# Attention weights kept in float32 for the AV product, and weight loads issued from POOL's queue

## The chip, the cores and the metric

The kernel runs on one core of a Trainium2 chip. A core has a matrix engine (TensorE, PE in the profile, with its weight loads shown as PEld), a vector engine (VectorE, DVE), a scalar engine (ScalarE, ACT), a general one (GpSimd, POOL) and a queue engine (SyncE, SP). Each works through its own instructions in order, and semaphores tie them together. Data lie in on-chip memory of 128 partitions; PE writes its results to a separate accumulation memory (PSUM). DMAs are issued from a queue of SP, ACT or POOL. The metric is device time in microseconds (us) of one execution.

## The reference

Four batches, eight heads, 768 positions, head size 64. Attention is restricted to clusters: every query and key is assigned to the nearest of 16 centroids of its head, and a query sees the keys of its own cluster only. The result goes through an MLP whose middle step mixes positions.

```python
mask = q_assign[:, :, :, None] == k_assign[:, :, None, :]
scores = scale * np.matmul(q, k.transpose(0, 1, 3, 2))
scores = np.where(mask, scores, -1000000000.0)
scores = scores - np.max(scores, axis=-1, keepdims=True)
attn = np.exp(scores)
attn = attn / (np.sum(attn, axis=-1, keepdims=True) + 1e-09)
attn_out = np.matmul(attn, v)
# x: the heads of attn_out side by side, (4, 768, 512)
h = np.maximum(x @ w_in, 0.0)              # w_in 512 x 1024
u, v = h[..., :512], h[..., 512:]
v_n = (v - mean(v)) / np.sqrt(var(v) + 1e-06)
v_s = np.einsum('ts,bsd->btd', w_spatial, v_n) + b_spatial[None, :, None]
return (u * v_s) @ w_out                   # w_out 512 x 512
```

All inputs and outputs are float32.

## The kernel before

Every float32 operand of a matrix product is split in two float16 halves, high and low, and a product is made of three of the four half-products: high-high, high-low and low-high. They accumulate in PSUM.

The work goes by pairs of heads, 16 pairs in all (four to a batch). For a pair, `prep` (L476) loads q, k and V, splits them, computes the cluster logits on PE (L508 to L510), turns them into one-hot rows on DVE and copies these as extra rows beside q, so that the mask is part of the score product. `shifts` (L577) runs the scores once (tile `tps`, one PSUM buffer, L587), takes each query's maximum on DVE (`nm`, L590), and lays the shift, again as extra rows, beside q. `attend` (L606) then does, for each of two heads, six key blocks: scores (tile `sc`, L622 and L624), exp on ACT into the float32 tile `p32` (L627), a cast to float16 on ACT (L628) and the low half on POOL (L629), both into `pt`. With all six blocks there, six AV blocks of 128 queries follow on PE (L638): for every key block three half-products of 65 columns (64 of V and a one, for the sum of the weights), with the weights as the stationary operand, and last a product with the tile `mean`, which adds the mean of V for rows where nothing is seen. The division (L653 to L655), the split of x (cast on DVE L657, low half on POOL L658) and a transposing DMA from SP (L660) put x into the buffer of its batch.

V is loaded to a staging tile `vraw` and split by ACT (L547) and DVE (L548). Its sum over positions is taken by PE: twelve matmuls with ones (L555, L556). DVE splits that (L564, L565), and two small DMAs put it in `mean`.

The MLP of a batch (`mlp`, L668) is 324 matmuls of 512 columns, all of L678, three half-products each. Its weights are loaded once, in 36 pieces; of a piece ACT makes the high half (L419, L440) and DVE the low one (L424, L445); for `w_in` and `w_out` DVE first puts the words of a float64 together (L434 to L436). The loads are issued from ACT's queue.

The order of all engines is worked out when the program is built: the class `Plan` (L114) simulates the queues with a cost for each step, and of the steps that are ready at a time it takes the one with the lowest key. Attention steps have small keys. The steps of the MLP on PE have keys from `FILLER` up, so they are taken only where nothing else is ready. The order on the chip is then fixed: an engine that waits for one instruction does not take a later one.

Of the kernel before, what the change touches and what calls it, by code (L numbers as in the profile page):

```python
# [7 lines left out]
F32 = mybir.dt.float32  # L8
F16 = mybir.dt.float16
# [6 lines left out]
P = 128  # L16
# [4 lines left out]
P_LOG = 10  # L21
V_SCALE = 2.0 ** 6
X_LOG = 10
# [5 lines left out]
PEN = 2.0 ** 15  # L29
MEAN_UNIT = 2.0 ** -2  # L30
LN2 = 0.6931471805599453
# [5 lines left out]
R_OH, R_SH, R_E, R_END = 64, 80, 81, 83  # L37
P32_BUFS = 3
PT_BUFS = 9
HQ_BUFS = 3  # L40
V_BUFS = 2
# [8 lines left out]
W_GAP = 4.0  # L50
W_ON = ('ACT',)
W_POOL = False
W_HI_DVE = ()
# [191 lines left out]
def kernel(  # L245
# [62 lines left out]
    r_raw = R(wk, "raw", [P, 2, S], F32, 1)  # L308
    r_vraw = R(wk, "vraw", [P, NT, P], F32, 1)
# [3 lines left out]
    r_pt = R(wk, "pt", [P, 2, S], F16, PT_BUFS)  # L313
    r_xhl = R(wk, "xhl", [P, NT, 2, P], F16, 1)
# [7 lines left out]
    r_nm = R(sm, "nm", [P, 2, NT], F32, 2)  # L322
    r_wh = R(sm, "wh", [2, 2, D + 2], F16, 2)
    r_wl = R(sm, "wl", [2, 2, D + 2], F16, 2)
    r_rc = R(sm, "rc", [P, NT], F32, 2)
# [150 lines left out]
    def prep(n):  # L476
# [5 lines left out]
        KV = PREP_KEY + 3.0  # L482
        raw, vraw = r_raw.new(), r_vraw.new()
# [50 lines left out]
        for x in range(4):  # L534
# [10 lines left out]
            else:  # L545
                rows.append(sp(lambda dst=dst, src=src: nc.sync.dma_start(out=dst(), in_=src()), 0.1, after=[tr, lg] + qa0, use=[hq, oht], key=KP))
        o_vh = op("ACT", 0.84, lambda: A.activation(out=vh.t[:, :, :, 0:D], in_=vraw.t.rearrange("p t (h d) -> p t h d", d=D), func=AF.Copy, scale=V_SCALE), after=[ldv, c_one], use=[vraw], new=[vh], key=KV)  # L547
        o_vl = op("DVE", 1.16, lambda: V.scalar_tensor_tensor(out=vh.t[:, :, :, D + 2:], in0=vraw.t.rearrange("p t (h d) -> p t h d", d=D), scalar=V_SCALE, in1=vh.t[:, :, :, 0:D], op0=ALU.mult, op1=ALU.subtract), after=[o_vh], use=[vraw, vh], key=KV)  # L548

        sv = r_acc.new()  # L550

        def sums():
            o = sv.t[:, 0:2 * (D + 2)].rearrange("p (h d) -> p h d", h=2)
            for t in range(NT):
                T.matmul(out=o[:, :, 0:D + 1], lhsT=ones, rhs=vh.t[:, t, :, 0:D + 1], start=(t == 0), stop=False, skip_group_check=True)  # L555
                T.matmul(out=o[:, :, 0:D], lhsT=ones, rhs=vh.t[:, t, :, D + 2:], start=False, stop=(t == NT - 1), skip_group_check=True)  # L556

        o = op("PE", 0.75, sums, after=[o_vh, o_vl, c_wt], use=[vh], new=[sv], cols=1548, key=KV)
        wh, wl = r_wh.new(), r_wl.new()

        def svr():
            return sv.t[0:2, 0:2 * (D + 2)].rearrange("p (h d) -> p h d", h=2)[:, :, 0:D + 1]

        h_ = op("DVE", 0.25, lambda: V.tensor_scalar(out=wh.t[:, :, 0:D + 1], in0=svr(), scalar1=MEAN_UNIT, scalar2=None, op0=ALU.mult), after=[o], use=[sv], new=[wh], key=KV)  # L564
        l_ = op("DVE", 0.3, lambda: V.scalar_tensor_tensor(out=wl.t[:, :, 0:D + 1], in0=svr(), scalar=MEAN_UNIT, in1=wh.t[:, :, 0:D + 1], op0=ALU.mult, op1=ALU.subtract), after=[h_], use=[sv, wh], new=[wl], key=KV)  # L565
        w1 = sp(lambda: nc.sync.dma_start(out=mw.t[R_E:R_E + 1, :, 0:D + 1], in_=wh.t[0:1, :, 0:D + 1]), 0.05, after=[h_, c_mean], use=[wh], new=[mw], key=KV)
        w2 = sp(lambda: nc.sync.dma_start(out=mw.t[R_E + 1:R_E + 2, :, 0:D + 1], in_=wl.t[0:1, :, 0:D + 1]), 0.05, after=[l_, c_mean], use=[wl, mw], key=KV)
        X["rows"] = rows + qa0
        X["go"] = rows + qa0 + [qa1, lo1]
        X["v"] = [o_vh, o_vl, w1, w2]  # L570

# [5 lines left out]
    def shifts(n):  # L577
# [22 lines left out]
        a = op("DVE", 0.2, lambda: V.tensor_scalar(out=cols(0, 1), in0=nmv(1), scalar1=PEN * PEN / 4, scalar2=1.0 / PEN, op0=ALU.min, op1=ALU.mult), after=tops + [c_sh], use=[nm], new=[sx], key=K_SH)  # L600
        e = op("DVE", 0.2, lambda: V.tensor_scalar(out=cols(1, 2), in0=nmv(2), scalar1=PEN * PEN / 2, scalar2=None, op0=ALU.is_gt), after=tops + [c_sh], use=[nm, sx], key=K_SH)
        tr = sp(lambda: nc.sync.dma_start_transpose(sht.t, sx.t.rearrange("p t c -> p (t c)")), 0.67, after=[a, e], use=[sx], new=[sht], turn=True, key=K_SH)
        X["shift"] = [sp(lambda h=h: nc.sync.dma_start(out=hq.t[R_SH:R_END, 1, h, :], in_=sht.t[R_SH + 16 * h:R_SH + 16 * h + 3].rearrange("c t s -> c (t s)")), 0.1, after=[tr], use=[hq, sht], key=K_SH) for h in range(2)]


    def attend(n):  # L606
# [5 lines left out]
        for h in range(2):  # L612
            pts, los = [], []
            for k in range(NT):
                sc, p32, pt = r_sc.new(), r_p32.new(), r_pt.new()
                pts.append(pt)

                def scores(sc=sc, h=h, k=k):
                    ks = slice(k * P, (k + 1) * P)
                    cols = (slice(0, 512), slice(512, S))  # L620
                    for cs in cols:
                        T.matmul(out=sc.t[:, cs], lhsT=lo.t[:, h, ks], rhs=hq.t[:, 2, h, cs], start=True, stop=False)  # L622
                    for cs in cols:
                        T.matmul(out=sc.t[:, cs], lhsT=hq.t[0:R_E, 0, h, ks], rhs=hq.t[0:R_E, 1, h, cs], start=False, stop=True)  # L624

                o = op("PE", 0.65, scores, after=X["go"] + X["shift"], use=[hq, lo], new=[sc], cols=2 * S, key=K_SC)
                o = op("ACT", 0.99, lambda sc=sc, p32=p32: A.activation(out=p32.t, in_=sc.t[:, 0:S], func=AF.Exp, bias=plog, scale=SC_UNIT), after=[o, m_half], use=[sc], new=[p32], key=K_EXP)  # L627
                o = op("ACT", 0.83, lambda pt=pt, p32=p32: A.copy(out=pt.t[:, 0, :], in_=p32.t), after=[o], use=[p32], new=[pt], key=K_HI)  # L628
                los.append(op("POOL", 1.7, lambda pt=pt, p32=p32: G_.tensor_tensor(out=pt.t[:, 1, :], in0=p32.t, in1=pt.t[:, 0, :], op=ALU.subtract), after=[o], use=[p32, pt], key=K_LO))  # L629
            av = r_acc.new()  # L630
            prev = None
            for t in range(NT):
                def values(av=av, pts=pts, h=h, t=t):
                    ts = slice(t * P, (t + 1) * P)
                    c = t * (D + 1)

                    def mm(w, lhsT, rhs, **k):
                        T.matmul(out=av.t[:, c:c + w], lhsT=lhsT, rhs=rhs, skip_group_check=True, **k)  # L638
# [7 lines left out]
                prev = op("PE", 0.62, values, after=los + X["v"] + [prev], use=pts + [vh, mw, hq] + ([av] if t else []), new=[] if t else [av], cols=18 * 65, key=AV_KEY)  # L646
            rc, xn = r_rc.new(), r_xn.new()
            f = 2.0 ** (6 - X_LOG)

# [6 lines left out]
            hs = slice(h * D, (h + 1) * D)  # L656
            o = op("DVE", 0.45, lambda xn=xn, hs=hs: V.tensor_copy(out=xhl.t[:, :, 0, hs], in_=xn.t), after=[o], use=[xn] + ([xhl] if h else []), new=[] if h else [xhl], key=K_X)  # L657
            xls.append(op("POOL", 1.0, lambda xn=xn, hs=hs: G_.tensor_tensor(out=xhl.t[:, :, 1, hs], in0=xn.t, in1=xhl.t[:, :, 0, hs], op=ALU.subtract), after=[o], use=[xn, xhl]))  # L658
# [162 lines left out]
```

## Time and profile before

| | |
|---|---|
| Median of 2 runs | 802.5 us (798.8 to 806.21) |
| The profiled execution | 808.25 us, its span 806.4 us |
| Mean granted clock of PE | 0.937 |
| PE busy | 669.5 us (83%) |
| DVE busy | 538.0 us (67%) |
| POOL busy | 430.5 us (53%), 330.9 of it L629 |
| ACT busy | 400.3 us (50%), 170.3 of it L627 and 152.7 L628 |

The profile is that of one execution. A row of a group gives line, engine, operation, tiles (out<-in), shape and count, then busy time in us, the mean of one in ns, and idle time ahead of them with what ended it. A row in order of time starts with start and length in us. A row of waits names who waited for whom, then us in total, how often, and the longest. The granted clock is 1 at full speed; it falls to half where PE has had little work. Busy times of PE hold the time until a result is written, so a busy PE may still have room. Before its first change the granted clock is shown as 1.

### The profile page before, as it was taken

What the parts mean: (1) busy time and instruction counts of PE and PEld (TensorE: products, weight loads), DVE (VectorE), ACT (ScalarE), POOL (GpSimd) and SP (SyncE); (2) the same over time, 40 slices, a digit from 0 to 9 for tenths busy, and PEclk for the clock granted to TensorE, in tenths of its full rate; (3) what the DMA queues carried; (4) which work ended last, traced back from release to release, by engine and by line L of the source; (5) the groups of instructions that cost most, each with busy time, mean ns of one, the idle gap of its engine ahead of it and who ended that gap; (6) DMA issues with size and microseconds to landing.
All of it is one profiled execution on the core that took longest, in us unless ns stands there. A gap on an engine that the chain in (4) does not pass through costs nothing. (4 is left out here: it accounts for less than half of the span.)

```text
span 806.4 us, 16781 instructions
## 1 busy us (share of the span) xinstructions
PE 669.5 (83%) x6865; PEld 398.6 (49%) x6865; DVE 538.0 (67%) x898; ACT 400.3 (50%) x541; POOL 430.5 (53%) x296
## 2 busy tenths in 40 slices
PE   2236867767678978999888979997999999999997
PEld 1113545444445554565655646555655655444443
DVE  6587797869896888677777787949767425312411
ACT  2016666637275647467737564766566771012111
POOL 1005665637374675758848385968476883212311
PEclk9999778767788999999999999999999999999999
DMA  4751144535243154054437240416412211121023
GB/s 154 166 139 53 37 115 113 141 80 164 59 118 51 30 112 122 16 72 136 84 108 157 67 106 18 119 26 152 99 42 57 64 48 21 27 79 53 12 52 92
DMA packets 96472, 67.74 MB, mean 84 GB/s; under 512 B 79310, under 2 KB 82060, under 8 KB 96396
## 3 DMA queue, kind: packets, MB, share of 16 engines
q1 hardware_dynamic: 87468, 51.34, 27.7%
q10 hardware_dynamic: 8928, 15.34, 5.9%
q8 instruction: 53, 0.87, 0.5%
q14 instruction: 23, 0.19, 0.1%
HBM read 27.63 MB, written 6.29 MB: 42 GB/s over the span
## 5 line engine op out<-in xcount | busy, mean ns | idle before, releaser
L629 POOL TENSOR_TENSOR pt<-p,pt 128x768 f16<-128x768 f32 x192 | 330.9, 1745 | 192.7 <-ACT pt L628 180.9
L590 DVE TENSOR_REDUCE nm<-tps 128x1 f32<-128x768 f32 x192 | 182.5, 950 | 94.2 <-PE tps L587 93.5
L627 ACT ACTIVATE p<-sc,plog 128x768 f32<-128x768 f32 x192 | 170.3, 900 | 86.1 <-PE sc L624 58.6
L587 PE MATMUL tps<-hq 80*128 80x512 f16 (+1 forms) x384 | 107.5, 366 | 90.2 <-DVE nm L590 79.0
L628 ACT CAST pt<-p 128x768 f16<-128x768 f32 x192 | 152.7, 830 | 34.4 <-PE acc L638 25.3
L638 PEld LDWEIGHTS <-pt 128*128 128x128 f16 x3456 | 132.9, 102 | 17.7 <-issue 4.5
L678 PE MATMUL acc<-win,xT 128*128 128x512 f16 x576 | 135.0, 386 | 2.5 <-DVE xn L655 2.2
L638 PE MATMUL acc<-vhl,pt 128*128 128x65 f16 (+1 forms) x3456 | 136.0, 199 | 0.5 <-POOL pt L629 0.5
L622 PE MATMUL sc<-hq,lo 128*128 128x512 f16 (+1 forms) x384 | 104.5, 356 | 10.6 <-ACT p L627 10.5
L624 PE MATMUL sc<-hq 81*128 81x512 f16 (+1 forms) x384 | 103.7, 354 | 6.2 <-DMA hq<-sht 6.2
L587 PEld LDWEIGHTS <-hq 80*128 80x128 f16 x384 | 37.9, 103 | 132.4 <-issue 103.8
L678 PE MATMUL acc<-vn,wsp 128*128 128x512 f16 x432 | 99.9, 379 | 0.5 <-DVE xn L655 0.5
L678 PEld LDWEIGHTS <-xT 128*128 128x128 f16 x576 | 56.3, 99 | 68.3 <-issue 5.2
L741 POOL TENSOR_TENSOR ghl<-u,ghl 128x512 f16<-128x512 f32 x24 | 29.4, 1226 | 73.6 <-DVE ghl L740 70.4
L678 PE MATMUL acc<-wou,gT 128*128 128x512 f16 x288 | 67.1, 379 | 1.0 <-DMA gT<-ghl 1.0
L678 PEld LDWEIGHTS <-wsp 128*128 128x128 f16 x432 | 41.6, 97 | 47.9 <-DVE xn L655 0.9
L624 PEld LDWEIGHTS <-hq 81*128 81x128 f16 x384 | 40.4, 105 | 38.5 <-issue 15.7
L739 DVE SCALAR_TENSOR_TENSOR u<-acc,bsp,u 128x512 f32<-128x512 f32 x24 | 18.0, 748 | 59.3 <-PE acc L678 59.2
L658 POOL TENSOR_TENSOR xhl<-xn,xhl 128x384 f16<-128x384 f32 x32 | 32.8, 1024 | 43.5 <-DVE xhl L657 34.6
L622 PEld LDWEIGHTS <-lo 128*128 128x128 f16 x384 | 35.8, 105 | 37.0 <-issue 17.4
L491 ACT ACTIVATE hq<-raw 128x768 f16<-128x768 f32 x32 | 26.0, 835 | 47.8 <-PE acc L638 24.7
L729 ACT ACTIVATE u<-acc 128x512 f32<-128x512 f32 x24 | 14.3, 596 | 71.3 <-PE acc L678 65.3
(87 smaller groups left out, 708.4 us busy)
## 6 DMA issues: line engine op xcount, KB each, us to landing
raw<-in_kqT_dram SPq DMA_DIRECT2D x15, 768.0 KB
vraw<-in_vp_dram SPq DMA_DIRECT2D x16, 384.0 KB
out_dram<-o ACTq DMA_DIRECT2D x24, 256.0 KB
hq<-hq SPq DMA_DIRECT2D x15, 384.0 KB
wraw<-in_w_in_dram ACTq DMA_DIRECT2D x16, 256.0 KB
hq<-lo SPq DMA_DIRECT2D x16, 192.0 KB
lo<-hq SPq DMA_DIRECT2D x16, 192.0 KB
wraw<-in_wsT_dram ACTq DMA_DIRECT2D x12, 192.0 KB
```

Of the source, the lines that this page charges most:

```text
L491: his.append(op("ACT", 0.83, lambda h=h: A.activation(out=hq.t[:, 0, h, :], in_=raw.t[:, h, :], func=AF.Copy, scale=QK_SCALE), after=[ld], ...
L587: T.matmul(out=sc.t[:, cs], lhsT=hq.t[0:R_SH, 1, h, t * P:(t + 1) * P], rhs=hq.t[0:R_SH, 0, h, cs], start=True, stop=True)
L590: tops.append(op("DVE", 0.92, lambda sc=sc, h=h, t=t: V.tensor_reduce(out=nm.t[:, h, t:t + 1], in_=sc.t[:, 0:S], axis=AX.X, op=ALU.max, ne ...
L622: T.matmul(out=sc.t[:, cs], lhsT=lo.t[:, h, ks], rhs=hq.t[:, 2, h, cs], start=True, stop=False)
L624: T.matmul(out=sc.t[:, cs], lhsT=hq.t[0:R_E, 0, h, ks], rhs=hq.t[0:R_E, 1, h, cs], start=False, stop=True)
L627: o = op("ACT", 0.99, lambda sc=sc, p32=p32: A.activation(out=p32.t, in_=sc.t[:, 0:S], func=AF.Exp, bias=plog, scale=SC_UNIT), after=[o, m ...
L628: o = op("ACT", 0.83, lambda pt=pt, p32=p32: A.copy(out=pt.t[:, 0, :], in_=p32.t), after=[o], use=[p32], new=[pt], key=K_HI)
L629: los.append(op("POOL", 1.7, lambda pt=pt, p32=p32: G_.tensor_tensor(out=pt.t[:, 1, :], in0=p32.t, in1=pt.t[:, 0, :], op=ALU.subtract), af ...
L638: T.matmul(out=av.t[:, c:c + w], lhsT=lhsT, rhs=rhs, skip_group_check=True, **k)
L658: xls.append(op("POOL", 1.0, lambda xn=xn, hs=hs: G_.tensor_tensor(out=xhl.t[:, :, 1, hs], in0=xn.t, in1=xhl.t[:, :, 0, hs], op=ALU.subtra ...
L678: T.matmul(out=acc.t, lhsT=lr[m][0], rhs=lr[m][1], start=(m == 0), stop=(m == n - 1))
L741: l = op("POOL", 1.12, lambda: G_.tensor_tensor(out=ghl.t[:, 1, :], in0=u32.t, in1=ghl.t[:, 0, :], op=ALU.subtract), after=[h], use=[u32, ...
```

## The change

The exp goes to a float32 tile, and that tile itself is the stationary operand of AV; there is no cast and no low half of the weights. V is loaded by DMA straight into the float32 tile `vhl`, whose 65th column holds ones, and is not split. An AV block has six float32 products of 65 columns and the product with `mean`. The tile `pt` is gone, and `p32` has 12 buffers.

The sum of V is made by POOL (five additions over the six blocks) and one float32 product with two columns of ones. Its low half is scaled by 2^11 in a third DVE step, and the row that picks it up in `shifts` by 2^-11, which makes two DVE steps of one.

The cast of x goes from DVE to ACT. The weight pieces of the MLP are loaded from POOL's queue; their low half is a subtraction on POOL, for which ACT scales the piece a second time. The first AV block of each head now also waits for the MLP's reading of the x buffer two batches earlier. Costs in the plan change with it.

```diff
-P32_BUFS = 3
-PT_BUFS = 9
+P32_BUFS = 12
...
-W_ON = ('ACT',)
-W_POOL = False
+W_ON = ('POOL',)
+W_POOL = True
...
-    ones = const.tile([P, P], F16, name="ones")
+    ones = const.tile([P, 2], F32, name="ones")
...
-    vhl = [const.tile([P, NT, 2, 2 * D + 2], F16, name="vhl%d" % i) for i in range(V_BUFS)]
+    vhl = [const.tile([P, NT, 2, D + 1], F32, name="vhl%d" % i) for i in range(V_BUFS)]
...
-        ldv = sp(lambda: nc.sync.dma_start(out=vraw.t, in_=vp[b, p]), 1.1, new=[vraw], key=KV)
+        ldv = sp(lambda: nc.sync.dma_start(out=vh.t[:, :, :, 0:D], in_=vp[b, p].rearrange("k t (h d) -> k t h d", h=2)), 1.1, after=[c_one], new=[vh], key=KV)
...
-        o_vh = op("ACT", 0.84, ...)
-        o_vl = op("DVE", 1.16, ...)
-        sv = r_acc.new()
+        sv, vs = r_acc.new(), r_vsum.new()
+        o = op("POOL", 0.4, lambda: G_.tensor_tensor(out=vs.t, in0=vh.t[:, 0], in1=vh.t[:, 1], op=ALU.add), after=[ldv], use=[vh], new=[vs], key=KV)
+        for t in range(2, NT):
+            o = op("POOL", 0.4, lambda t=t: G_.tensor_tensor(out=vs.t, in0=vs.t, in1=vh.t[:, t], op=ALU.add), after=[o], use=[vh, vs], key=KV)
...
-            for t in range(NT):
-                T.matmul(out=o[:, :, 0:D + 1], lhsT=ones, rhs=vh.t[:, t, :, 0:D + 1], start=(t == 0), stop=False, skip_group_check=True)
-                T.matmul(out=o[:, :, 0:D], lhsT=ones, rhs=vh.t[:, t, :, D + 2:], start=False, stop=(t == NT - 1), skip_group_check=True)
+            T.matmul(out=sv.t[0:2, 0:2 * (D + 1)], lhsT=ones, rhs=vs.t.rearrange("p h d -> p (h d)"), start=True, stop=True)
...
-        e = op("DVE", 0.2, lambda: V.tensor_scalar(out=cols(1, 2), in0=nmv(2), scalar1=PEN * PEN / 2, scalar2=None, op0=ALU.is_gt), ...)
+        es = [op("DVE", 0.2, lambda c=c: V.tensor_scalar(out=cols(c, 1), in0=nmv(1), scalar1=PEN * PEN / 2, scalar2=2.0 ** (-MEAN_LOG * (c - 1)), op0=ALU.is_gt, op1=ALU.mult), ...) for c in (1, 2)]
...
-                o = op("ACT", 0.99, lambda sc=sc, p32=p32: A.activation(out=p32.t, in_=sc.t[:, 0:S], func=AF.Exp, bias=plog, scale=SC_UNIT), ...)
-                o = op("ACT", 0.83, lambda pt=pt, p32=p32: A.copy(out=pt.t[:, 0, :], in_=p32.t), ...)
-                los.append(op("POOL", 1.7, lambda pt=pt, p32=p32: G_.tensor_tensor(out=pt.t[:, 1, :], in0=p32.t, in1=pt.t[:, 0, :], op=ALU.subtract), ...))
+                los.append(op("ACT", 0.9, lambda sc=sc, p32=p32: A.activation(out=p32.t, in_=sc.t[:, 0:S], func=AF.Exp, bias=plog, scale=SC_UNIT), ...))
...
-                        mm(D + 1, pts[k].t[:, 0, ts], vh.t[:, k, h, 0:D + 1], start=(k == 0), stop=False)
-                        mm(D, pts[k].t[:, 0, ts], vh.t[:, k, h, D + 2:], start=False, stop=False)
-                        mm(D + 1, pts[k].t[:, 1, ts], vh.t[:, k, h, 0:D + 1], start=False, stop=False)
+                        mm(D + 1, pts[k].t[:, ts], vh.t[:, k, h, :], start=(k == 0), stop=False)
...
-                prev = op("PE", 0.62, values, after=los + X["v"] + [prev], ..., cols=18 * 65, key=AV_KEY)
+                prev = op("PE", 0.75, values, after=los + X["v"] + [prev] + (xread.get(b - 2, []) if t == 0 else []), ..., cols=24 * 65, key=AV_KEY)
...
-            o = op("DVE", 0.45, lambda xn=xn, hs=hs: V.tensor_copy(out=xhl.t[:, :, 0, hs], in_=xn.t), ...)
+            o = op("ACT", 0.5, lambda xn=xn, hs=hs: A.copy(out=xhl.t[:, :, 0, hs], in_=xn.t), ...)
```

More of the change, by code (lines that the diff above doesn't have):

```diff
@@ L308 @@
     r_raw = R(wk, "raw", [P, 2, S], F32, 1)
-    r_vraw = R(wk, "vraw", [P, NT, P], F32, 1)
+    r_vsum = R(wk, "vsum", [P, 2, D + 1], F32, 1)
     r_oht = R(wk, "oht", [P, NT, P], F16, 1)
@@ L482, in prep @@
         KV = PREP_KEY + 3.0
-        raw, vraw = r_raw.new(), r_vraw.new()
+        raw = r_raw.new()
         if n == 0:
@@ L566, in prep @@
[L566 to L567 removed]
+            T.matmul(out=sv.t[0:2, 0:2 * (D + 1)], lhsT=ones, rhs=vs.t.rearrange("p h d -> p (h d)"), start=True, stop=True)
+        o = op("PE", 0.25, sums, after=[o, c_wt], use=[vs], new=[sv], cols=520, key=KV)
@@ new lines, in prep @@
+        wh, w32, wl = r_wh.new(), r_w32.new(), r_wl.new()
+        def svr():
+            return sv.t[0:2, 0:2 * (D + 1)].rearrange("p (h d) -> p h d", h=2)
+        h_ = op("DVE", 0.25, lambda: V.tensor_copy(out=wh.t, in_=svr()), after=[o], use=[sv], new=[wh], key=KV)
+        l_ = op("DVE", 0.3, lambda: V.tensor_tensor(out=w32.t, in0=svr(), in1=wh.t, op=ALU.subtract), after=[h_], use=[sv, wh], new=[w32], key=KV)
+        l_ = op("DVE", 0.2, lambda: V.tensor_scalar(out=wl.t, in0=w32.t, scalar1=2.0 ** MEAN_LOG, scalar2=None, op0=ALU.mult), after=[l_], use=[w32], new=[wl], key=KV)
@@ L568, in prep @@
+        w1 = sp(lambda: nc.sync.dma_start(out=mw.t[R_E:R_E + 1, :, 0:D + 1], in_=wh.t[0:1]), 0.05, after=[h_, c_mean], use=[wh], new=[mw], key=KV)
+        w2 = sp(lambda: nc.sync.dma_start(out=mw.t[R_E + 1:R_E + 2, :, 0:D + 1], in_=wl.t[0:1]), 0.05, after=[l_, c_mean], use=[wl, mw], key=KV)
         X["rows"] = rows + qa0
         X["go"] = rows + qa0 + [qa1, lo1]
-        X["v"] = [o_vh, o_vl, w1, w2]
+        X["v"] = [ldv, w1, w2]
     xdone = {}
@@ L656, in attend @@
             hs = slice(h * D, (h + 1) * D)
-            o = op("DVE", 0.45, lambda xn=xn, hs=hs: V.tensor_copy(out=xhl.t[:, :, 0, hs], in_=xn.t), after=[o], use=[xn] + ([xhl] if h else []), new=[] if h else [xhl], key=K_X)
+            o = op("ACT", 0.5, lambda xn=xn, hs=hs: A.copy(out=xhl.t[:, :, 0, hs], in_=xn.t), after=[o], use=[xn] + ([xhl] if h else []), new=[] if h else [xhl], key=K_X)
             xls.append(op("POOL", 1.0, lambda xn=xn, hs=hs: G_.tensor_tensor(out=xhl.t[:, :, 1, hs], in0=xn.t, in1=xhl.t[:, :, 0, hs], op=ALU.subtract), after=[o], use=[xn, xhl]))
```

33 lines of the change are left out of this document (11 added, 22 removed).

## The prediction

> **What bounds the kernel now.** I read the busy times by stretch first, cut where the work changes, then the waits of TensorE (PE), then the chain that ended last.
>
> ```profile
> 0.00:81.00 81.00, 31.97 (x216) 15.95 (x217) 58.49 (x135) 22.85 (x33) 14.43 (x19) 0.98 0.48 127
> 81.00:240.00 159.00, 114.23 (x1390) 76.36 (x1389) 134.74 (x194) 95.97 (x136) 92.20 (x56) 0.77 0.39 100
> 240.00:669.00 429.00, 390.57 (x4639) 246.27 (x4638) 308.03 (x477) 261.76 (x340) 292.15 (x193) 0.97 0.35 81
> 669.00:806.00 137.00, 132.75 (x628) 60.02 (x624) 36.72 (x93) 19.71 (x33) 31.74 (x30) 1.00 0.18 49
> PE tps L587 <- DVE nm L590: 79.0, 63, 3.7
> PE sc L622 <- ACT p L627: 10.5, 5, 3.4
> PE acc L638 <- POOL pt L629: 0.5, 2, 0.3
> 669.48 126.92 PE acc L678 x588
> 81.00:240.00 159.00, 3.16 (x8) 1.17 (x9) 0.77 0.39 100
> L629 POOL TENSOR_TENSOR pt<-p,pt 128x768 f16<-128x768 f32 x192 | 330.9, 1745 | 192.7 <-ACT pt L628 180.9
> L628 ACT CAST pt<-p 128x768 f16<-128x768 f32 x192 | 152.7, 830 | 34.4 <-PE acc L638 25.3
> ```
>
> The columns of the stretches are length, then busy time of PE, weight load, DVE, ACT and POOL, granted clock, DMA share and GB/s; the later row of 81 to 240 is that of the MLP's line L678 alone (PE, weight load). From 669 us on nothing but the MLP's matmuls is left: 588 of its 1296 in 126.92 us, 0.216 us each. MLP work fills holes of PE during attention, and what finds no hole is done at the end. So the time is PE's work plus PE's holes, wherever they lie. The holes are before 240 us, where next to no MLP work is ready yet (8 matmuls): there PE idles 49 + 45 us and has a clock of 0.77 in the second stretch. What ends its waits is DVE (79.0 us), hardly ever ACT or POOL (10.5 and 0.5), so taking the 331 us of L629 from POOL is worth nothing directly. What counts is DVE, 134.7 of 159 us busy in the second stretch, and PE itself.
>
> **AV on PE.** These are pieces of the chain (start, length, work, count):
>
> ```profile
> 627.88 0.58 PE acc L638 x19
> 628.46 0.33 PE sc L622 x2
> 628.79 0.33 PE sc L624 x2
> 629.70 0.33 PE tps L587 x2
> 312.02 0.22 PE L555 MATMUL acc<-vhl,ones 128*128 128x130 f16 x1
> 312.67 0.22 PE L556 MATMUL acc<-vhl,ones 128*128 128x128 f16 x1
> ```
>
> A block of AV is 18 half-products and the mean row: 0.58 us, or 30.6 ns each with the weight load hidden; 192 blocks cost 111 us. The change makes it 6 float32 products and the mean row. No such product is in the trace. The nearest row is the one float32 matmul, a transpose at the start:
>
> ```profile
> 6.71 0.18 PEld L391 LDWEIGHTS acc<-p 128*128 128x128 f32 x1 [6.71 <-DVE p L388]
> 6.71 0.47 PE L391 MATMUL acc<-p 128*128 128x128 f32 x1 [6.71 <-DVE p L388]
> 7.54 0.10 PEld L508 LDWEIGHTS <-hq 128*128 128x128 f16 x1 [0.65 <-ACT hq L491]
> 12.72 0.27 PE L556 MATMUL acc<-vhl,ones 128*128 128x128 f16 x1 [0.90 <-DVE vhl L548]
> 12.78 0.32 PE L555 MATMUL acc<-vhl,ones 128*128 128x130 f16 x1
> 12.89 0.31 PE L556 MATMUL acc<-vhl,ones 128*128 128x128 f16 x1
> ```
>
> Two f16 matmuls start 0.11 us apart there, against 0.65/11 = 0.059 at 312 us, so this is half clock. The float32 load took 0.08 us more than an f16 one, 0.04 at full clock. The float32 matmul took 0.20 more than the f16 one of equal size: 0.08 of load, 0.12 or about one more pass. Lower bound: two passes, 2 x 30.6 = 61 ns a product, a block of 6 x 0.061 + 0.031 = 0.40 us, 76 us in all (35 fewer). Upper bound: four passes, each with its own longer load in the open, 4 x (30.6 + 40) = 282 ns, 1.73 us a block, 331 us (220 more). I take four passes with hidden loads: two halves of each operand give four half-products, of which the kernel now does three (high-high, high-low, low-high), and the diff's own count of columns goes from 18 to 24. That is 4 x 30.6 = 122 ns, 0.763 us a block, 146.5 us: **35 us more**. Hidden, because all 18 f16 loads of a block are hidden, and two loads longer by 40 ns still fit under four passes. The sum over V was twelve matmuls in 0.70 us (312.02 to 312.67, and one step) per pair; it becomes one float32 product of 130 columns, 4 x 0.059 = 0.24: **7 us less** over 16 pairs.
>
> The Trainium skill, TensorE: Matmul & The Clock Gate, section Weight-path perf modes, says that the fast weight load is on only where the type is not FP32; the longer load at 6.71 agrees. By its section on LDWEIGHTS (columns / 1.2 ns, so 107 ns for 128), four loads in a row would bind a product at 428 ns, an estimate; a block would be 2.6 us and the sum near 1,085. I keep hidden loads as the likeliest, since the trace shows every load of this loop running ahead, and make the open load a rival.
>
> **What DVE loses in the second stretch.** Its groups there, with mean ns, and one place that shows why they are slow:
>
> ```profile
> L493 DVE SCALAR_TENSOR_TENSOR lo<-raw,hq 128x768 f16<-128x768 f32 x8 | 13.1, 1633 | 0.0
> L435 DVE SCALAR_TENSOR_TENSOR top<-wraw,top 128x256 uint32<-128x256 uint32 x14 | 13.0, 931 | 0.2
> L424 DVE SCALAR_TENSOR_TENSOR wsp<-wraw,wsp 128x384 f16<-128x384 f32 x12 | 11.7, 978 | 6.5 <-ACT wsp L419 6.5
> L436 DVE SCALAR_TENSOR_TENSOR top<-wraw,top 128x256 uint32<-128x256 uint32 x14 | 9.2, 659 | 0.2
> L434 DVE TENSOR_SCALAR top<-wraw 128x256 uint32<-128x256 uint32 x14 | 8.1, 577 | 0.2
> L657 DVE CAST xhl<-xn 128x384 f16<-128x384 f32 x8 | 8.0, 1005 | 0.0
> L445 DVE SCALAR_TENSOR_TENSOR wou<-top,wou 128x256 f16<-128x256 f32 x7 | 5.5, 784 | 1.7 <-ACT wou L440 1.7
> L445 DVE SCALAR_TENSOR_TENSOR win<-top,win 128x256 f16<-128x256 f32 x8 | 4.9, 617 | 1.8 <-ACT win L440 1.8
> L548 DVE SCALAR_TENSOR_TENSOR vhl<-vraw,vhl 128x768 f16<-128x768 f32 x4 | 4.4, 1091 | 0.0
> 129.50 5.24 POOL L629 TENSOR_TENSOR pt<-p,pt 128x768 f16<-128x768 f32 x3
> 131.50 1.75 DVE L436 SCALAR_TENSOR_TENSOR top<-wraw,top 128x256 uint32<-128x256 uint32 x1
> 133.71 0.90 ACT L627 ACTIVATE p<-sc,plog 128x768 f32<-128x768 f32 x1 [3.05 <-DVE top L436]
> 134.66 0.80 PE L622 MATMUL sc<-hq,lo 128*128 128x512 f16 x2 [3.19 <-ACT p L627]
> ```
>
> Removed outright: L424 11.7, L657 8.0, L445 5.5 + 4.9, L548 4.4, together 34.5 us (the weights' low halves go to POOL, the cast to ACT). And beside POOL's L629 DVE's own steps stretch: L436 took 1.75 us under the 5.24 us run of POOL, and ACT and then PE waited 3 us behind it. With L629 gone I put L493, L435, L436 and L434 at what they took at other places:
>
> ```profile
> 124.72 0.41 DVE L436 SCALAR_TENSOR_TENSOR top<-wraw,top 128x256 uint32<-128x256 uint32 x1
> 122.79 0.41 DVE L435 SCALAR_TENSOR_TENSOR top<-wraw,top 128x256 uint32<-128x256 uint32 x1
> 122.35 0.28 DVE L434 TENSOR_SCALAR top<-wraw 128x256 uint32<-128x256 uint32 x1
> 459.94 0.95 DVE L493 SCALAR_TENSOR_TENSOR lo<-raw,hq 128x768 f16<-128x768 f32 x1
> ```
>
> That is 8 x 0.68 + 14 x (0.52 + 0.25 + 0.30) = 20 us. The second `is_gt` and the third step on the mean add under 1 us a pair, 3 here. DVE comes to 134.7 - 34.5 - 20 + 3 = 83 us for four pairs. PE's work for a pair is 12 x (0.33 + 0.33 + 0.33 + 0.763) = 21 and some 1.5 of small matmuls, 90 for four: PE is now the fuller one. DVE's 134.7 filled a stretch of 159, a factor of 1.18; 90 x 1.18 = 106, and I take 110. **49 us less**, AV's extra work of these pairs included.
>
> **The other stretches.** Before 81 us DVE loses eight low halves and two V steps: 4 us less. From 240 to 669 PE has 429 - 390.6 = 38 us of holes and about 12 of lower clock; I take half of the 50, 25 less, as DVE's 72% there falls too. Against it stand AV's extra of twelve pairs, 12 x 12 x 0.183 = 26, less 5 of V sums: together **4 us less**. The end from 669 on is only moved.
>
> Costed at nothing: ACT loses its cast of p and of V, gains the 32 casts of x and a second scaling of 36 weight pieces, each no longer than a cast of p (0.83), so at most 56 us against the 152.7 lost with L628 alone. Its cover gone, a cast of x would wait behind one exp (0.90). POOL gains the low halves, 36 issues of DMAs and five additions of 130 elements a pair; even at 1 us each that is 152 us against the 331 lost, and the first use of the weights is the MLP, after four pairs. On SP the load of V now waits until the AV of two pairs before has read its tile, where it waited for a staging tile; behind it in SP's order stand the row copies and shifts of the next pair, and a wait of 1 us there delays scores by 1 us. V's rows of 64 go in 256-byte pieces, 1536 for 128 before; AV needs them half a pair later. I allow 0 to 10 us for SP in all and take 0.
>
> **Sum.** 808.25 - 49 - 4 - 4 = 751 in the profiled execution; that one stands 0.7% above the median of 802.5, so 746.
>
> **The rivals.** *The likeliest case* has hidden loads: 746, between 705 (three passes, 35 less, and the second stretch at 105) and 785 (the stretch at 125, and none of the 25 gained after 240). Chance 0.60.
>
> *One float32 load in the open per product.* 162 ns, 192 x 6 x 0.04 = 46 us more; some 8 of it fall into holes of the second stretch: 784. For it: the single float32 pair, where matmul and load share their start. Chance 0.12.
>
> *Loads in the open, and the kernel slower.* Two loads or more a product, at L638: 202 ns with two, 92 us over the likeliest case, less about 15 that fall into holes, so 823; with four, 282 ns, 184 more less 15, 915. It decides from about 1.5 open loads (184 ns), where 71 us more eat the 56 gained. For it: the longer load, and that a 65-column pass is too short to cover one by itself (30.6 against 40 more than now). Against it: no load of this loop shows as a wait today. The rule of the Trainium skill on the fast load belongs here. Chance 0.20.
>
> *PE's holes stay.* If the chain from tops to maximum and back, on one PSUM tile, keeps its pace, PE waits for DVE as before and AV's 28 us net are added: 836, or 830 by the median. For it: 79.0 us of waits on L590, and L590 itself is untouched. Against it: those waits include others' steps in between, which shrink. Chance 0.08.
>
> **Numbers.** This measurement tells 2% from no change, 786 to 819. Faster: the likeliest case nearly whole (0.55) and half of the second (0.06), 0.61. Same: 0.05 + 0.06 + 0.02, 0.13. Slower: 0.26. The range of 80% goes from 705 to 845, which takes in two open loads and the kept holes and leaves out four loads; the likeliest case's own is 705 to 785.
>
> **What would show it.** Right: a block of AV at 0.70 to 0.80 us in the chain; L436 near 0.41 on average; MLP matmuls in numbers from about 190 us on, where now 8 come before 240; PE's waits on L590 well below 79. Wrong: AV blocks of 1.2 us or more, or weight loads of float32 filling the loop; DVE still over 80% before 240; or a long wait on SP's queue at the load of V.

## The result and the profile after

The changed kernel takes **869.5 us** (median of 2 runs, 868.26 to 870.76) against 802.5: a ratio of 1.0835 [1.061, 1.106], slower. The forecast was 746, on the other side. The profiled execution took 868.26 us, its span is 866.5, the mean granted clock 0.958 (before 0.937). The lines of the code have moved a little: AV is now L633, the MLP L671, `tps` L584, `nm` L587, the load of V L486.

Busy times of the page after, and then the stretches cut at the same places as before, plus the end (length, busy time of PE, weight load, DVE, ACT, POOL, clock, DMA share, GB/s):

```profile
PE 795.0 (92%) x5553; PEld 535.0 (62%) x5553; DVE 406.5 (47%) x846; ACT 278.2 (32%) x401; POOL 182.5 (21%) x256
```

```profile
0.00:81.00 81.00, 40.52 (x297) 24.12 (x298) 54.44 (x134) 24.86 (x41) 21.77 (x46) 1.00 0.50 126
81.00:240.00 159.00, 137.14 (x1126) 105.54 (x1125) 91.33 (x181) 72.66 (x116) 50.88 (x78) 0.89 0.45 108
240.00:669.00 429.00, 425.27 (x3163) 303.10 (x3163) 213.97 (x420) 146.29 (x191) 73.42 (x99) 0.97 0.33 73
669.00:806.00 137.00, 137.00 (x721) 77.68 (x720) 33.12 (x79) 26.61 (x40) 23.67 (x23) 0.94 0.18 42
...
81.00:215.80 134.80, 112.94 (x934) 85.88 (x933) 80.46 (x160) 62.51 (x102) 48.63 (x75) 0.87 0.51 123
```

DVE, ACT and POOL are all relieved: DVE has 406.5 us of work where it had 538.0. From 240 us on PE has no holes left (425.3 of 429, where it had 390.6). Before 240 us it idles 62.3 us, where it idled 93.8. The last row ends where the first MLP matmul starts, at 215.8 us (before: 234.1): there DVE has 80.5 us of work and PE 112.9. The time went up all the same, so PE's own work has grown. The costliest groups of the page, and pieces of the chain of waits (start, length, work, count), show where:

```profile
L633 PEld LDWEIGHTS acc<-vhl,p 128*128 128x128 f32 x2304 | 283.3, 200 | 12.7 <-issue 2.0
L633 PE MATMUL acc<-vhl,p 128*128 128x65 f32 x2304 | 286.7, 282 | 0.0
```

```profile
227.70 2.72 PE acc L633 x26
...
428.44 5.18 PE acc L633 x26
...
593.34 16.70 PE acc L633 x156
...
726.18 129.51 PE acc L671 x600
```

There are 1152 float32 products (192 blocks of six) and **2304 records**: a product is two weight loads and two matmuls. A block is 13 records, so two blocks take 2.72 us and one 1.36, where the forecast had 0.763. Less 0.031 for the mean row that is 0.222 us a product, two records of 111 ns. In 192 blocks it is (1.36 - 0.763) x 192 = 115 us above the forecast; the profiled execution is 868 - 751 = 117 above the sum made for it. That these two nearly agree is partly chance, since other terms were off as well (see the table further down). At 428 us the same two blocks took 5.18 us: the clock was 0.50 there, although PE was busy for all of the 16 us from 424 to 440 (just before, at 422.5, it had waited 1.0 us). The last piece is the MLP's rest, 600 matmuls now against 588.

What the forecast wanted from DVE did happen. The groups of DVE and PE between 81 and 215.8 us, and the waits of PE and SP:

```profile
L491 DVE SCALAR_TENSOR_TENSOR lo<-raw,hq 128x768 f16<-128x768 f32 x8 | 8.2, 1030 | 0.0
L433 DVE SCALAR_TENSOR_TENSOR top<-wraw,top 128x256 uint32<-128x256 uint32 x12 | 5.0, 417 | 0.2
L434 DVE SCALAR_TENSOR_TENSOR top<-wraw,top 128x256 uint32<-128x256 uint32 x12 | 5.0, 417 | 0.2
...
L633 PE MATMUL acc<-mean,hq 83*128 83x65 f16 x42 | 8.2, 195 | 0.0
```

```profile
PE tps L584 <- DVE nm L587: 33.2, 25, 3.0
...
SPq L486 <- PE acc L633: 34.2, 8, 10.7
```

The steps that stood at 931, 659 and 1633 ns beside POOL's low half of the weights are at 417, 417 and 1030. PE's waits for the maximum fell from 79.0 to 33.2 us.

### The profile page after: what moved, and what is told of

Its sections match the earlier page's. It is cut to its first block, busy times and chain, and to the rows that moved or that the text cites. A ratio compares the mean times of both kernels' runs of the same rounds, so it can differ in the third digit from the quotient of the medians.

```text
span 866.5 us, 13638 instructions
## 1 busy us (share of the span) xinstructions
PE 795.0 (92%) x5553; PEld 535.0 (62%) x5553; DVE 406.5 (47%) x846; ACT 278.2 (32%) x401; POOL 182.5 (21%) x256
## 4 chain that ended last, share of the span: by engine, by line
PE 81%; DMA 8%; DVE 4%; POOL 3%; ACT 2%; issue 1%; SPq 0%; ACTq 0%; POOLq 0%
PE acc L633 32%; PE acc L671 29%; PE sc L619 6%; PE sc L621 6%; PE tps L584 6%; DMA vhl<-in_vp_dram 4%; DMA raw<-in_kqT_dram 2%; DVE nm L587 2%; POOL vsum L549 2%; DMA hq<-sht 1%; DVE lo L491 1%; ACT hq L489 1%; ACT p L624 1%; DMA wraw<-in_wsT_dram 1%; DMA gT<-ghl 0%
## 5 line engine op out<-in xcount | busy, mean ns | idle before, releaser
L633 PEld LDWEIGHTS acc<-vhl,p 128*128 128x128 f32 x2304 | 283.3, 200 | 12.7 <-issue 2.0
L633 PE MATMUL acc<-vhl,p 128*128 128x65 f32 x2304 | 286.7, 282 | 0.0
L587 DVE TENSOR_REDUCE nm<-tps 128x1 f32<-128x768 f32 x192 | 183.3, 955 | 172.8 <-PE tps L584 171.8
L624 ACT ACTIVATE p<-sc,plog 128x768 f32<-128x768 f32 x192 | 166.5, 898 | 115.6 <-PE sc L621 87.5
L584 PE MATMUL tps<-hq 80*128 80x512 f16 (+1 forms) x384 | 104.2, 356 | 37.9 <-DVE nm L587 33.2
L671 PE MATMUL acc<-win,xT 128*128 128x512 f16 x576 | 131.7, 379 | 0.6 <-ACT v L692 0.6
L619 PE MATMUL sc<-hq,lo 128*128 128x512 f16 (+1 forms) x384 | 98.6, 339 | 6.7 <-ACT p L624 6.3
L671 PE MATMUL acc<-vn,wsp 128*128 128x512 f16 x432 | 100.7, 385 | 0.0
L621 PE MATMUL sc<-hq 81*128 81x512 f16 (+1 forms) x384 | 97.7, 336 | 2.4 <-DMA hq<-sht 2.4
L671 PEld LDWEIGHTS <-xT 128*128 128x128 f16 x576 | 55.9, 97 | 64.7 <-issue 0.8
L584 PEld LDWEIGHTS <-hq 80*128 80x128 f16 x384 | 35.2, 103 | 68.0 <-issue 45.6
L671 PEld LDWEIGHTS <-wsp 128*128 128x128 f16 x432 | 42.6, 99 | 50.6 <-issue 3.0
L671 PE MATMUL acc<-wou,gT 128*128 128x512 f16 x288 | 68.5, 384 | 1.8 <-DMA gT<-ghl 1.8
L646 DVE TENSOR_SCALAR rc<-acc 128x6 f32<-128x6 f32 x32 | 5.3, 165 | 107.3 <-PE acc L633 107.3
L650 ACT CAST xhl<-xn 128x384 f16<-128x384 f32 x32 | 16.2, 506 | 114.3 <-DVE xn L648 79.6
L671 PEld LDWEIGHTS <-gT 128*128 128x128 f16 x288 | 28.2, 99 | 34.7 <-DMA gT<-ghl 2.3
```

The costliest lines, as they stand in the source:

```text
L584: T.matmul(out=sc.t[:, cs], lhsT=hq.t[0:R_SH, 1, h, t * P:(t + 1) * P], rhs=hq.t[0:R_SH, 0, h, cs], start=True, stop=True)
L587: tops.append(op("DVE", 0.92, lambda sc=sc, h=h, t=t: V.tensor_reduce(out=nm.t[:, h, t:t + 1], in_=sc.t[:, 0:S], axis=AX.X, op=ALU.max, ne ...
L624: los.append(op("ACT", 0.9, lambda sc=sc, p32=p32: A.activation(out=p32.t, in_=sc.t[:, 0:S], func=AF.Exp, bias=plog, scale=SC_UNIT), after ...
L671: T.matmul(out=acc.t, lhsT=lr[m][0], rhs=lr[m][1], start=(m == 0), stop=(m == n - 1))
```

## The experiments

The theory after the result: a float32 product loads its stationary operand twice, by the slow way, and these loads, not the matmuls, set its 222 ns. The rivals: the matmul itself passes slowly; the order is wrong, because the plan was told 0.75 us for a block that takes 1.36; or another part of the change (weights on POOL, the sum of V, the waits of SP) costs what DVE gave. Times of before are medians of runs on the same chip: 804.4, 807.2 and 804.5 for the three groups of runs.

### Fewer columns of V, fewer columns of weights

`cols33` multiplies only 33 columns of V for the key blocks 1 to 5; `rows64` loads only 64 of the 128 query columns of the weights there. Both leave out that part of AV.

```diff
 for k in range(NT):
-    mm(D + 1, pts[k].t[:, ts], vh.t[:, k, h, :], start=(k == 0), stop=False)
+    if k == 0: mm(D + 1, pts[k].t[:, ts], vh.t[:, k, h, :], start=True, stop=False)
+    # cols33:
+    else: T.matmul(out=av.t[:, c + 32:c + 65], lhsT=pts[k].t[:, ts], rhs=vh.t[:, k, h, 32:65], ...)
+    # rows64:
+    else: T.matmul(out=av.t[0:64, c:c + 65], lhsT=pts[k].t[:, t * P:t * P + 64], rhs=vh.t[:, k, h, :], ...)
```

> For key blocks 1 to 5 the float32 AV product is made of columns 32 to 64 of V only, 33 instead of 65 (the other columns of these blocks are left out). The changed kernel takes two records (load and matmul) per product and 1.37 us per AV block. Theory 'load in the open': a record is a load of 128 columns (53 ns at 2.4 GHz) and then two passes over the columns; 32 columns fewer take 2 x 13.3 = 27 ns from each of ten records, so a block takes 1.10 us and the kernel 869 - 51 = 818 us. Rival 'slow passes, load hidden': the record goes with the columns, 111 x 33 / 65 = 56 ns, a block 0.82 us and the kernel 764. Rival 'fixed cost per record': 1.37 us and 869.

> For key blocks 1 to 5 the float32 AV product has 64 queries as stationary columns instead of 128 (the other 64 queries of each block get key block 0 and the mean row only). Theory 'load in the open': each of ten loads gets 64 columns shorter, 27 ns, so a block takes 1.10 us and the kernel 818 us. Rivals 'slow passes, load hidden' and 'fixed cost per record': a block stays at 1.37 us and the kernel at 869.

Measured: `cols33` **1018.6 us**, clock 0.795; `rows64` **794.3 us**, clock 0.976 (one run each). The chain and one stretch of `cols33`:

```profile
820.52 2.08 PE acc L639 x10
...
851.83 1.09 PE acc L639 x10
...
240.00:669.00 429.00, 425.26 (x2617) 313.21 (x2616) 191.03 (x365) 128.21 (x167) 60.45 (x81) 0.76 0.29 68
```

The same of `rows64`:

```profile
642.22 0.73 PE acc L639 x10
...
240.00:669.00 429.00, 425.73 (x3450) 271.90 (x3448) 215.71 (x429) 154.47 (x204) 78.20 (x101) 1.00 0.35 73
```

With half the columns of V a record stays at 109 ns where the clock is full (1.09 / 10). With half the columns of weights it falls to 73. So the load sets the record, and what streams past is hidden under it. `rows64` halves the rows of the result too, but `cols33` makes about half of the result as well, and its record stays. The theory that load and matmul stand one behind the other is refuted (it wanted 27 ns less, 84, for a record of `cols33`), and so are slow passes (56 ns). The times of the two kernels can't decide this, because the clock differs. The Trainium skill, TensorE: Matmul & The Clock Gate, section LDWEIGHTS, has columns / 1.2 ns: 107 for 128 columns agrees with each of the two records; 53 for 64 columns does not cover the 73, and what sets those is open. The expectations missed both times: `rows64` came out at 794 where 818 was the nearest, and none had that of `cols33`, which has less work and takes 149 us more than the changed kernel. The stretch shows why: PE is busy for 425 of 429 us, and the clock is 0.76. At half clock ten records take 2.08 us.

### Twice the columns of V

`f32_both` multiplies each weight block with V of both heads, 130 columns; half of that is never read. If loads set the time, this is free, and if the clock goes by the columns that stream, it rises.

```diff
-mm(D + 1, pts[k].t[:, ts], vh.t[:, k, h, :], start=(k == 0), stop=False)
+blocks = av.t[:, 0:7 * (D + 1)].rearrange("p (b c) -> p b c", c=(D + 1))
+both = blocks[:, 0:t + 2:t + 1] if h else blocks[:, t:7:6 - t]
+T.matmul(out=both, lhsT=pts[k].t[:, ts], rhs=vh.t[:, k], ...)
```

> The changed kernel, each float32 AV product with the columns of both heads of V (130 instead of 65; the other head's half goes to a spare place and is not used). The run with 33 columns showed a record that stays near 107 ns and a clock of 0.795. Theory 'the load of 128 float32 columns sets the record, and the granted clock follows the columns that stream': a block stays within 1.37 to 1.45 us, the clock rises from 0.958 to over 0.98, the kernel comes to 840 to 865. Rival 'columns cost': two passes of 65 more, 27 ns each, 12 to a block, 62 us more, 930.

Measured: **860.8 us**, ratio 1.067 [1.0619, 1.0721], clock 0.979. A piece of its chain and the stretch from 240 to 669:

```profile
712.83 1.43 PE acc L638 x12
...
240.00:669.00 429.00, 425.74 (x3206) 303.88 (x3205) 215.96 (x428) 146.79 (x192) 74.56 (x100) 1.00 0.34 73
```

Twelve records take 1.43 us, 119 ns each against 111: twice the columns cost at most some 8 ns. If a record made two passes, 130 columns would take 2 x 59 = 118 ns (an estimate from the float16 row at 312.02 of the kernel before), so it is open whether the load still sets the record at this width. The whole is not slower than the changed kernel. Beside it the changed kernel's row for 240 to 669 (above) and that of `cols33` make a series: PE is busy for 425.3, 425.3 and 425.7 us, and the clock is 0.76 with 33 columns a load, 0.97 with 65 and 1.00 with 130. The last step of this series says little, as `w_act` below will show.

### The rest of the change without float32 products

`f16_stand` keeps everything else and makes AV of 18 float16 products again. The exp goes straight to float16, V is cast by ACT, and the low halves are left out of the computation (the high half stands in their place, so that AV has as many products on PE as before).

```diff
-r_p32 = R(wk, "p32", [P, S], F32, P32_BUFS)
+r_ph = R(wk, "ph", [P, S], F16, P32_BUFS)
...
+o_v16 = op("ACT", 0.84, lambda: A.activation(out=v16.t, in_=vh.t, func=AF.Copy, scale=1.0), after=[ldv], ...)
...
 mm(D + 1, pts[k].t[:, ts], vh.t[:, k, h, :], start=(k == 0), stop=False)
+mm(D, pts[k].t[:, ts], vh.t[:, k, h, 0:D], start=False, stop=False)
+mm(D + 1, pts[k].t[:, ts], vh.t[:, k, h, :], start=False, stop=False)
...
-prev = op("PE", 0.75, values, ..., cols=24 * 65, key=AV_KEY)
+prev = op("PE", 0.62, values, ..., cols=18 * 65, key=AV_KEY)
```

> The changed kernel, but the exp writes a float16 tile, V is cast to float16 by ACT (16 casts), and AV has 18 float16 products a block as before (low halves are left out, the high one stands in for them): the price of a float32 product is taken away, the rest of the change stays. Theory 'only the price of AV was wrong': a block takes 0.58 us and the kernel 869 - 192 x 0.79 = 717, up to 735 where the time turns into holes of PE. Rival 'something else of the change costs too' (the order, the weights on POOL's queue, the load of V on SP): 760 or more.

Measured: **731.1 us** (725.65 to 736.16), ratio 0.9101 [0.9029, 0.9173], clock 0.965. A piece of its chain (three blocks), the MLP's first product (count, shortest, mean and longest in ns, first start and last end in us), and a wait:

```profile
136.64 1.75 PE acc L638 x57
...
L678 PE MATMUL acc<-win,xT x576: 376/379/390, 191.8 to 690.6; 128*128 128x512 f16 x192
...
PE acc L557 <- POOL vsum L554: 14.3, 6, 6.3
```

The time lies in the 717 to 735 that were expected if only the price of AV was wrong. With AV back at 0.58 us a block the rest of the change is worth 804.4 - 731.1 = 73 us (with 16 casts of V on ACT that the change itself does not have). The float32 product alone then costs 869.5 - 731.1 = 138, of 192 x (1.36 - 0.58) = 150 us of added work at full clock. These two numbers are the result: -73 and +138. The last row is a wait of 14.3 us that the forecast had at nothing: PE's product with ones stands at the head of its queue until POOL has summed V.

### The plan's cost of a block

`true_cost` tells the plan 1.37 us for a block.

```diff
-prev = op("PE", 0.75, values, ..., cols=24 * 65, key=AV_KEY)
+prev = op("PE", 1.37, values, ..., cols=24 * 65, key=AV_KEY)
```

> The changed kernel, but the plan is told 1.37 us for an AV block, as measured, instead of 0.75; no instruction changes, only the order. Theory 'PE's work': the same work in another order, 855 to 880 us. Rival 'the order made from the wrong cost is what costs': below 850.

Measured: **886.1 us**, ratio 1.0985 [1.0942, 1.1027], clock 0.934. The second stretch, and the MLP's first product:

```profile
81.00:240.00 159.00, 149.77 (x1081) 119.53 (x1080) 87.57 (x171) 71.87 (x113) 51.03 (x76) 0.78 0.45 106
...
L671 PE MATMUL acc<-win,xT x576: 376/379/381, 290.6 to 851.1; 128*128 128x512 f16 x192
```

A wrong cost in the plan is not where the time went: with the right one the kernel is no faster (the two intervals overlap, and the time lies a little beyond what was expected). MLP work starts 75 us later, and the second stretch runs at 0.78 instead of 0.89 although PE is busier.

### The weights part, undone and alone

`w_act` puts the weight pieces back on ACT's queue with their low halves on DVE; `b_wpool` makes that part of the change alone, in the kernel before.

```diff
 # w_act, against the changed kernel; b_wpool is the reverse, against the kernel before
-W_ON = ('POOL',)
-W_POOL = True
+W_ON = ('ACT',)
+W_POOL = False
```

> The changed kernel with the weights' part undone: loads from ACT's queue, low halves on DVE. Theory 'PE's work is the loss, the weights' part helps a little': DVE gets 26 us of steps back in the first 240 us, beside a fuller PE: 869 to 885. Rival 'POOL's queue or POOL's halves delay the start of the MLP or of attention': 860 or less.

> The kernel before with only the weights' part of the change: loads from POOL's queue, low halves on POOL. The changed kernel got 1% faster when this part was undone. Theory 'POOL's own steps beside DVE are what costs DVE': 36 more steps of POOL (0.7 to 1 us, some 30 us) for 26 us of DVE taken away, in a stretch where POOL is already busy with the low halves of the weights: 795 to 815, no difference. Rival 'DVE's steps in the first 240 us set the time': 25 us less, 780.

Measured: `w_act` **860.2 us**, ratio 1.0634 [1.0563, 1.0705], clock 0.979; `b_wpool` **806.3 us**, ratio 1.0026 [0.9991, 1.0062], clock 0.923. Alone, the part makes no difference. Undone, it is not told apart from the changed kernel (its interval overlaps 1.061 to 1.106); it came out below what the theory gave, at the edge of the rival (860 or less). The clock from 240 us on is 1.00 in its profiled execution, which was the fastest of its four, against 0.97:

```profile
240.00:669.00 429.00, 422.31 (x3216) 300.00 (x3216) 219.86 (x422) 144.89 (x191) 74.24 (x100) 1.00 0.34 73
```

So with 65 columns a load another order alone gives the clock that `f32_both` has with 130. Of the 34.5 us of work that DVE lost in the second stretch, 22 are these low halves, and moving them was worth little by itself. Which of the other parts the 73 us come from is not shown, since they were not undone one by one; the end of POOL's long subtraction is a candidate.

### One load a product: float32r

Here the operands of AV are of the type float32r: exp writes the weights so, rounded, and ACT casts V; V has 66 columns, and there are 10 weight tiles. `f32r_both` has the 132 columns of both heads.

```diff
+r_ph = R(wk, "ph", [P, S], mybir.dt.float32r, 10)
+r_vh16 = R(wk, "vh16", [P, NT, 2, D + 2], mybir.dt.float32r, 1)
...
+o_v16 = op("ACT", 0.84, lambda: A.activation(out=v16.t, in_=vh.t, func=AF.Copy, scale=1.0), after=[ldv], ...)
...
-mm(D + 1, pts[k].t[:, ts], vh.t[:, k, h, :], start=(k == 0), stop=False)
+mm(D + 2, pts[k].t[:, ts], vh.t[:, k, h, :], start=(k == 0), stop=False)
```

> The changed kernel with the operands of AV in the type float32r, rounded by the exp and by a cast of V on ACT (the lowest bits of weights and V are left out), 66 columns, 10 weight tiles. Theory 'load in the open', with one load and one pass per product: 53 + 28 + 3 = 84 ns, a block 0.53 us, the kernel about 710. If it takes two passes: 111 ns, 0.70 us, 740. Rival 'as slow as float32 at so few columns': 1.37 us and 869.

> The float32r kernel, each AV product with the columns of both heads (132 instead of 66; the other head's half is not used). Theory 'load sets the record, clock follows streaming columns': a block stays at 0.72 to 0.76 us, the mean clock rises from 0.893 to 0.96 or more, and the kernel falls from 785 to 710 to 740 us, although PE is given more work. Rival 'columns cost': 28 ns more per product, 32 us, 817.

Measured: `f32r` **784.8 us**, ratio 0.9804 [0.9718, 0.989], clock 0.893; `f32r_both` **782.1 us**, ratio 0.9649 [0.9566, 0.9733], clock 0.915. Pieces of the chain and two stretches of `f32r`:

```profile
83.41 2.56 PE acc L638 x14
...
544.86 4.23 PE acc L638 x42
...
81.00:240.00 159.00, 146.43 (x945) 102.99 (x945) 100.02 (x195) 84.77 (x132) 53.36 (x82) 0.72 0.51 122
240.00:669.00 429.00, 416.21 (x2694) 257.12 (x2693) 220.89 (x447) 162.31 (x220) 82.58 (x103) 0.91 0.32 72
```

One record a product now: 42 records (six blocks) in 4.23 us, 0.705 a block and 112 ns a product. So it is the number of loads that makes the price, 111 ns each. The expectation had a product of 111 ns as well, but as a load of 53 and two passes, a sum that `cols33` refutes; that number was hit by luck. The block lies close to the 0.763 that the forecast had taken for another reason, and yet the kernel takes 785 and not 746: the clock is 0.72 in the second stretch, where PE is busy for 146 of 159 us, and two blocks take 2.56 us there. With twice the columns the clock is 0.915, where 0.96 or more was expected, and the time is not told apart from that of `f32r` (the intervals overlap), where 710 to 740 was expected. The theory that the clock follows the columns missed here.

Three more kernels start from `f32r_both`: `f32r_wact` undoes the weights part, `f32r_cols` tells the plan how many columns really stream (857 a block where it had 1560; the plan keeps account of PE's columns to choose filler work), `f32r_wact_cols` does both.

```diff
 # f32r_wact                     # f32r_cols
-W_ON = ('POOL',)
-W_POOL = True
+W_ON = ('ACT',)
+W_POOL = False
...
-cols=24 * 65
+cols=6 * 132 + 65
```

> The float32r kernel with the columns of both heads, and the weights' part undone (loads from ACT's queue, low halves on DVE). Theory 'the weights' part costs 1% in this order too': 770 to 778 against 782. Rival 'what it showed on the changed kernel came from the clock that the order happened to get (0.979 against 0.958)': between 775 and 800, and whichever way goes with the mean clock against 0.915.

> The float32r kernel with the columns of both heads, and the plan told the columns that stream in an AV block (6 x 132 + 65 = 857 instead of 1560), from which it reckons where the clock falls. No instruction changes, only the order. Theory 'the loss left is half clock in the stretches with little but AV' (134 us of half clock): an order that reckons with it mixes MLP work in and comes to 765 to 780, clock 0.93 or more. Rival 'before the first MLP work there is nothing to mix in': 780 to 790, clock unchanged at 0.91 to 0.92.

> Both of the last two edits together, as the version meant to beat both kernels: 755 to 775 us if they add, 775 to 790 if the stretch before the first MLP work is what is left.

| | us | ratio to before | clock |
|---|---|---|---|
| `f32r_wact` | 766.7 | 0.9486 [0.94, 0.9573] | 0.935 |
| `f32r_cols` | 796.0 | 0.9896 [0.9834, 0.9957] | 0.906 |
| `f32r_wact_cols` | **758.3** | 0.9405 [0.9333, 0.9478] | 0.948 |

The last one beats both kernels. Its time lies in the 755 to 775 that were expected if the two edits add up, but they do not add up, so that was luck. Its second and third stretch, and its longest wait of PE beside that for the maximum:

```profile
81.00:240.00 159.00, 135.37 (x936) 94.12 (x935) 109.15 (x224) 73.11 (x106) 24.27 (x38) 0.81 0.53 121
240.00:669.00 429.00, 420.50 (x2827) 262.82 (x2826) 224.54 (x445) 166.15 (x221) 85.50 (x102) 0.98 0.34 75
```

```profile
PE acc L557 <- POOL vsum L554: 22.6, 7, 6.5
```

Against `f32r` the clock is 0.81 and 0.98 instead of 0.72 and 0.91. The single edits do not explain it: the columns edit made `f32r_both` slower by itself and, on top of the weights part, the kernel no slower and perhaps faster (the intervals overlap). Neither expectation of `f32r_cols` held, and `f32r_wact` came out faster than either of its own. In the changed kernel's chain POOL's weight steps stand between the sum of V and DVE's next steps (from 96 us on), which would be a reason for the weights part; that was not tried by itself, and the effect stays open. Some of what is left to gain shows in the last row: 22.6 us in which PE stands behind POOL's sum of V.

## Why the prediction was wrong

**The step that failed** is in the part on AV: "I take four passes with hidden loads", and its reason, "Hidden, because all 18 f16 loads of a block are hidden, and two loads longer by 40 ns still fit under four passes". The runs showed the reverse: two records a product, and in each the matmul is hidden under the load. A record is 111 ns with 65 columns, 109 with 33, 119 with 130, and 73 with half the weights. The 0.08 us had been read from one float32 load that stood by itself, as its difference to a float16 load. Halved for full clock that is 40 ns; the reason quoted counts these 40 ns alone as a load's price, without what a load takes to begin with, and the upper bound sets them on a pass of 30.6 and has 70 ns. Back to back a load takes 109 to 111. The passes (30.6) were a true number, and not the one that binds; how many passes a record makes is not shown.

In us, with the measured split:

| | forecast | measured |
|---|---|---|
| a block of AV | 0.763 | 1.36 |
| float32 products against float16 ones, in all | +35 | +138 (869.5 - 731.1) |
| everything else | -92 (57 + 35) | -73 (804.4 - 731.1) |
| sum | -57 | +65 to +67 |

**The bounds** of the product, 61 to 282 ns, hold the measured 222. **The rival** "loads in the open, and the kernel slower" was right in sign and nearly in size: with two loads it had 202 ns and 823 us, and the point from which it decides, 184 ns, was passed. Its mechanism was not: loads are not added to the passes. The range, 705 to 845, left out 869, because two loads were priced at 40 ns more than now and not at a full load each.

The rule that fast weight load is not for FP32 (the Trainium skill, TensorE: Matmul & The Clock Gate, section Weight-path perf modes) fits the runs: a float32 record, which its load sets, takes 111 ns, and a float16 product with its load took 30.6. The page's price of a load would have given 2 x 107 = 213 ns for two loads, an estimate; the prediction had it for four (1,085 us). It was set aside because no load of the loop showed as a wait.

In the changed kernel the loads show hardly any wait either (12.7 us of idle time before 283.3 of work): a load that binds does not show as idle time of PE. PEld's share does not tell it either. From 593 to 610 us, where AV runs alone, PEld is busy for 16.95 of 17.00 us; but in the float16 block at 627.88 of the kernel before it was busy for 0.52 of 0.58. What told it is the time from record to record, which stayed when the columns were halved and fell when the weights were.

**DVE in the second stretch** was right: 83 us forecast for four pairs, 80.5 measured up to 215.8 us; L434 at 417 ns (0.41), L491 at 1030 (0.95). The stretch itself was to take 110 us and took 134.8; 42 blocks of AV lie in it, and 42 x 0.6 = 25 would make up the difference. So MLP matmuls start at 215.8 and not near 190; in `f16_stand` they start at 191.8.

**The holes after 240** were to give half of 50: PE's idle time there fell from 38 to 3.7 us, more than was taken; the clock stayed at 0.97.

**Costed at nothing**, and not nothing: the way of V. SP's load waits 34.2 us for AV to have read the tile (eight times, up to 10.7), then come the transfer and five additions, and PE's product with ones stands behind them; the changed kernel's chain goes through it:

```profile
88.80 4.60 DMA vhl<-in_vp_dram
93.39 0.02 issue
93.42 0.02 POOLq L547
93.44 0.44 issue
93.88 0.43 POOL vsum L547
```

PE itself waits little for that sum in the changed kernel (2.9 us), but 14.3 us in `f16_stand`. This is a candidate for part of the 19 us by which everything else fell short; no run takes it away, and the rest is not taken apart. The rival that PE's holes stay is refuted (33.2 us of waits on the maximum).

## What to carry to other kernels

Before a product's type is changed, ask what its stationary operand costs to load, back to back, and compare that with the columns that stream past it: with few columns the load is the price, and hiding goes the other way round. A load that binds is not found among the waits, and not in PEld's share: count the records per product, and take the time from one to the next. And a change that relieves every other engine is worth only what PE's holes hold (73 us here); that can't pay for 150 us more of PE's own work.

## What the runs showed of the hardware

A PE that never stops can fall to half clock, so having had little work is not the only case. From 835 to 876 us of `cols33` PE was busy all the time (41.0 of 41.0 us). Up to 851 there are MLP matmuls among the rest and the clock is 1.00; then it is mostly AV with 33 columns, and some scores; the clock is 0.98 up to 866 and 0.50 from there to 876. Ten records that took 1.09 us at 851.83 (above) take

```profile
866.32 2.08 PE acc L639 x10
```

With 65 columns it goes both ways: in the changed kernel 156 records ran alone from 593.34 for 16.7 us, and the clock was 1.00; from 428 to 440 it stayed at 0.50. From 240 to 669 us the profile has PE busy for 425 us or more in `cols33`, the changed kernel and `f32_both`, and the granted clock was 0.76, 0.97 and 1.00 for 33, 65 and 130 columns a load. Only the first step is clear of the order of the work, since 65 columns came to 1.00 in `w_act` (422.3 us busy) and to 0.94 in `true_cost` (417.9 us).

The Trainium skill, TensorE: Matmul & The Clock Gate, section What's actually happening, ties the clock to how busy PE has been. The profile's busy time does not tell the three kernels apart. But it holds the time until a result is written (282 ns for a record, where the next one starts after 111), so these runs can't say that the page is wrong, only that this busy time is not what the clock goes by. What would fit is that time spent loading weights does not count as activity and columns that stream do; this is argued, not shown. Against columns alone speaks `f32r_both`, which streams 132 columns a load, one record a product, and has a lower clock than the changed kernel: 0.74 against 0.89 in the second stretch and

```profile
240.00:669.00 429.00, 412.18 (x2703) 259.79 (x2701) 222.91 (x449) 162.55 (x220) 83.37 (x104) 0.94 0.32 72
```

against 0.97 after it, with 17 us of idle PE there. Useless columns cost no time in `f32_both` (860.8 against 869.5).

A float32r product of 128 weight columns is one record of 112 ns, a float32 one two of 111, and a record with 64 weight columns took 73 and not half of 109.
